# The low part of 22 of 64 weight tiles made by GpSimd instead of an adding DMA

## The chip, the core and the metric

The kernel runs on one core of a Trainium2 chip. The metric is the device time of an execution in microseconds, and the median of several executions. TensorE does the matrix products, VectorE and ScalarE the elementwise work, GpSimd elementwise work and the issue of DMAs that do arithmetic, SyncE (SP) the issue of the plain DMAs. Rows call them PE, DVE, ACT, POOL and SP; PEld is the loading of a stationary operand.

## What is computed

A retention layer (linear attention with a decaying state, batch 2, 8 heads, 768 positions, head width 64) gives 1536 rows of 512, and two feed-forward layers follow, each with a hidden width of 2048. All four weight matrices come in as 8-byte floats.

```python
state = gamma * state + outer(k[t], v[t]); y[t] = scale * q[t] @ state     # per batch and head
x = y.transpose(0, 2, 1, 3).reshape(1536, 512)
g = softplus(x @ w1_in);      x = g @ w1_out                               # first layer
h = x @ w2_in
out = (h * clip(h + 3, 0, 6) / 6) @ w2_out                                 # second layer
```

## The kernel before

**Matrix products in parts.** Every operand of the large products is kept as a high part, rounded to TensorE's fast format, and a low part, what the rounding left out. A product is three matmuls: high by high, high by low, low by high. For activations the parts are `hi` and `lo` (`x_hi` and `x_lo` between layers), for weights the two halves of one tile `w_parts`: `t[:, 0]` high, `t[:, 1]` low.

**Weights.** A matrix is cut into 16 tiles of 128 x 512 numbers, so there are 64. A tile is named by (m, o, f): layer m, o = 0 for the layer's first matrix and 1 for its second, f from 0 to 15. `fetch` has SyncE load the raw words of a tile into one of three `raw` buffers. `convert` makes 4-byte floats of them: ScalarE scales `raw` (L89), VectorE clamps it (L90, called the `raw` step below) and makes the word `w` in three steps, one with one input (L91) and two with two (L92, L93). `w` lies in one of two buffers, so the tile after next can start its `w` only when all that reads this one is done. Then the parts: ScalarE writes minus the rounded `w` to the low half (L95), a DMA that GpSimd issues adds `w` to it in place (L96), and ScalarE writes the rounded `w` to the high half (L97).

**The order of tiles.** `order` (L104 to L107) has four tiles of the first layer's first matrix, then one of the second and one of the first by turns, then the second layer's 32. `feed(n)` converts up to n of them; `done[1]` counts those converted.

**Steps and units.** The attention runs in 12 units of 128 rows (`unit`). The first four come alone, and the others stand ahead of the first steps of the feed-forward layers. A step (`step`) is one f for one chunk of 512 rows: `gemm1`, twelve matmuls of 512 columns, whose result goes through ScalarE and VectorE (`g`, `e`, then `hi` and `lo`), and `gemm2`, twelve matmuls with the `hi` and `lo` of two steps earlier (`LAG`). In chunk 0 of the first layer `lo` is made by GpSimd (L352), elsewhere by VectorE. Steps of chunk 0 feed the weight tiles, mostly two each. In a unit, VectorE multiplies the scores by a mask (`pt`, L213), on which TensorE's next products wait (`pt,vs`), and writes `on` and `bd`; GpSimd makes `vs`, `bd` and `x_lo`.

**What sets the order.** Each engine works through its own queue in order. Up to the first two tiles (`feed(2)`, L302) the queues stand as the code is written; after that (`nc.on = False`) a scheduler merges what the code gives into the queues when the program is built, by its own estimates of durations.

Of the kernel before, what the change touches and what calls it, by code (L numbers as in the profile page):

```python
# [10 lines left out]
F32 = mybir.dt.float32  # L11
F32R = mybir.dt.float32r
U32 = mybir.dt.uint32
AF = mybir.ActivationFunctionType
ALU = mybir.AluOpType
# [25 lines left out]
@with_exitstack  # L41
def kernel(ctx, tc, q, k, v, w1_in, w1_out, w2_in, w2_out, tq, tk, tc_, tg, out):
    nc = InOrder(tc)
    B, H, S, D = q.shape
    NT, DM = out.shape
    DFF = w1_in.shape[1]
    NP = H // 2
    KD = DM // P
    NF = DFF // P
    C = P  # L50
    NCH = S // C
    CH = 512
    chunks1 = [(0, 0, 512), (1, 0, 512), (2, 0, 512)]
    chunks2 = [(0, 0, 512), (1, 0, 512), (2, 0, 512)]
    LAG = 2
    EARLY = 4

    tc.nc.scalar.preload_act_table_set("softplus")

    xpool = ctx.enter_context(tc.tile_pool(name="xpool", bufs=1))  # L60
    x_hi = [xpool.tile([P, KD, CH], F32R, name=f"x_hi{c}") for c in range(NT // CH)]
    x_lo = [xpool.tile([P, KD, CH], F32R, name=f"x_lo{c}") for c in range(NT // CH)]

    win_p = ctx.enter_context(tc.tile_pool(name="win", bufs=NF))
    wout_p = ctx.enter_context(tc.tile_pool(name="wout", bufs=NF))
    psum = ctx.enter_context(tc.tile_pool(name="psum", bufs=1, space=PSUM))
    raw_p = ctx.enter_context(tc.tile_pool(name="raw", bufs=3))
    cv_p = ctx.enter_context(tc.tile_pool(name="cv", bufs=2))

    w_in_t, w_out_t, raws = {}, {}, {}  # L70
    words = {0: (w1_in.bitcast(U32), w1_out.bitcast(U32)), 1: (w2_in.bitcast(U32), w2_out.bitcast(U32))}

    def fetch(m, o, f):
        raw = raw_p.tile([P, CH, 2], U32, tag="raw", name="raw")
        src = words[m][o]
        if o:
            nc.sync.dma_start(out=raw.rearrange("p n t -> p (n t)"), in_=src[f * P:(f + 1) * P, :])
        else:
            nc.sync.dma_start(out=raw.rearrange("p (k n) t -> p k (n t)", k=KD),
                              in_=src[:, 2 * f * P:2 * (f + 1) * P].rearrange("(k p) f -> p k f", p=P))  # L80
        raws[m, o, f] = raw

    def convert(m, o, f):

        raw = raws.pop((m, o, f))
        low, y = raw[:, :, 0], raw[:, :, 1]

        w = cv_p.tile([P, CH], U32, tag="w", name="w")
        nc.scalar.activation(y.bitcast(F32), y.bitcast(F32), AF.Copy, scale=2.0 ** -112)  # L89
        nc.vector.tensor_scalar(y.bitcast(F32), y.bitcast(F32), -TOP, TOP, ALU.max, ALU.min)  # L90
        nc.vector.tensor_scalar(w, y, 3, None, ALU.logical_shift_left)  # L91
        nc.vector.scalar_tensor_tensor(w, y, 0x80000000, w, ALU.bitwise_and, ALU.bitwise_or)  # L92
        nc.vector.scalar_tensor_tensor(w, low, 29, w, ALU.logical_shift_right, ALU.bitwise_or)  # L93
        t = (wout_p if o else win_p).tile([P, 2, CH], F32R, tag="w", name="w_parts")
        nc.scalar.activation(t[:, 1], w.bitcast(F32), AF.Copy, scale=-1.0)  # L95
        nc.gpsimd.dma_start(out=t[:, 1].bitcast(F32), in_=w.bitcast(F32), accum_op=ALU.add)  # L96
        nc.scalar.activation(t[:, 0], w.bitcast(F32), AF.Copy)  # L97
        if o:
            w_out_t[m, f] = t
        else:  # L100
            w_in_t[m, f] = t.rearrange("p a (k n) -> p a k n", k=KD)

    NU = B * NCH
    order = [(0, 0, f) for f in range(EARLY)]  # L104
    for f in range(NF):
        order += [(0, 1, f)] + [(0, 0, f + EARLY)] * (f + EARLY < NF)
    order += [(1, 0, f) for f in range(NF)] + [(1, 1, f) for f in range(NF)]  # L107
    done = [0, 0]

    def fetch_weights(n):  # L110
        while done[0] < min(len(order), n):
            fetch(*order[done[0]])
            done[0] += 1

    def feed(n):

        n = min(n, len(order))
        while done[1] < n:
            fetch_weights(done[1] + (1 if nc.on else 2))
            convert(*order[done[1]])  # L120
            done[1] += 1

    banks = psum.tile([P, 8, CH], F32, name="banks")
    free = list(range(8))

    def bank(hold=False):

        i = free.pop(0)
        if not hold:
            free.append(i)  # L130
            return banks[:, i, :]
        return i, banks[:, i, :]

    def release(i):
        free.append(i)

    def first(f):
        return EARLY + 2 * (f + 1) - max(0, f + 1 + EARLY - NF)

    step, last, n_steps = moe(ctx, tc, nc, out, x_hi, x_lo, w_in_t, w_out_t, chunks1, chunks2, NF, KD, DM, CH, LAG, feed, first, bank, release)  # L140
    s = 0
    with ExitStack() as actx:
        unit = attention(actx, tc, nc, q, k, v, tq, tk, tc_, tg, x_hi, x_lo, CH, bank, feed, fetch_weights)
        for u in range(CH // P, NU):
            unit(u)
            step(s)
            s += 1
    while s < n_steps:
        step(s)
        s += 1  # L150
# [298 lines left out]
```

## Time and profile before

| | us |
|---|---|
| median of 3 runs | 633.73 (632.96 to 635.1) |
| the profiled execution | 632.11 |
| its span, first to last instruction | 630.3 |
| TensorE busy in the span | 600.6 (95%) |
| VectorE busy | 352.4 (56%) |
| ScalarE busy | 281.1 (45%) |
| GpSimd busy, DMA issues counted | 116.5 (18%) |
| mean granted TensorE clock | 0.984 of full speed |

The shares are means over the whole span; VectorE and GpSimd have most of their work in the first 200 us. The time outside the span is 1.8 us. A busy TensorE isn't TensorE at its peak: where its clock is granted at half, the same matmul is busy for longer.

### The profile page before, as it was taken

The page shows a single profiled execution, that of the slowest core. Times are in us where ns is not written, and L with a number is a line of the kernel's source. Part 1 is how long each engine was busy: PE and PEld are TensorE (multiplying, and loading weights), DVE is VectorE, ACT ScalarE, POOL GpSimd, SP SyncE. Part 2 cuts the span into 40 slices and gives each one's busy share as a digit, 9 for nine tenths or more (in the row PEclk, how much of TensorE's full clock was granted, in tenths as well). Part 3 has the DMA queues.
Part 4 walks back from the last instruction along what each step waited for, and adds up shares of the span by engine and source line. Part 5 has one row for each costly group of instructions (what it writes and reads, how often), then busy time and mean ns, then how long its engine had stood idle before and what let it go on. Part 6 is the DMA issues. An engine that isn't in the chain of part 4 may idle for free.

```text
span 630.3 us, 7793 instructions
## 1 busy us (share of the span) xinstructions
PE 600.6 (95%) x2963; PEld 493.1 (78%) x2963; DVE 352.4 (56%) x567; ACT 281.1 (45%) x481; POOL 116.5 (18%) x126
## 2 busy tenths in 40 slices
PE   7957979799989999999999999999999999999997
PEld 6846767678768888888887878888888888888886
DVE  4569988898856333357576789932232222422223
ACT  3327556667655333356556677832222222222221
POOL 1735655444420000011111122300000000000000
PEclk9979979799999999999999999999999999999999
DMA  9988986798750000025558688810010000100001
GB/s 193 227 230 222 255 212 152 185 214 203 168 131 1 0 1 0 1 43 125 113 138 216 151 203 218 198 33 1 0 68 0 1 0 2 68 0 1 0 1 67
DMA packets 70662, 63.70 MB, mean 101 GB/s; under 512 B 40160, under 2 KB 56800, under 8 KB 70624
## 3 DMA queue, kind: packets, MB, share of 16 engines
q1 hardware_dynamic: 61408, 46.42, 25.5%
q0 software_dynamic: 9216, 16.78, 16.1%
q8 instruction: 23, 0.38, 0.3%
q14 instruction: 15, 0.12, 0.1%
HBM read 43.26 MB, written 3.15 MB: 74 GB/s over the span
## 4 chain that ended last, share of the span: by engine, by line
PE 60%; DVE 10%; issue 6%; DMA 4%; ACT 4%; POOL 1%; DVEq 0%; POOLq 0%; ACTq 0%
PE banks L31 60%; DVE w L31 5%; DMA raw<-in_moe_w_in_dram 3%; DVE raw L31 2%; ACT w_parts L31 1%; DVE g L31 1%; ACT e L31 1%; DMA w_parts<-w 1%; DVE e L31 1%; ACT raw L31 1%; ACT hi L31 1%; POOL lo L31 1%; DVE lo L31 1%; DVE pt L31 0%; POOL w_parts L31 0%
## 5 line engine op out<-in xcount | busy, mean ns | idle before, releaser
L31 PE MATMUL banks<-x_hi,w_parts 128*128 128x512 f32 x768 | 255.2, 393 | 5.5 <-DMA w_parts<-w 5.5
L31 PEld LDWEIGHTS banks<-x_hi,w_parts 128*128 128x128 f32 x768 | 145.0, 189 | 36.4 <-DMA w_parts<-w 5.7
L31 PE MATMUL banks<-x_lo,w_parts 128*128 128x512 f32 x384 | 150.2, 391 | 0.0
L31 PE MATMUL banks<-hi,w_parts 128*128 128x512 f32 x384 | 127.0, 392 | 0.7 <-ACT hi L31 0.4
L31 PE MATMUL banks<-w_parts,hi 128*128 128x512 f32 (+1 forms) x386 | 118.5, 388 | 0.5 <-DVE g L31 0.5
L31 DVE SCALAR_TENSOR_TENSOR w<-raw,w 128x512 uint32<-128x512 uint32 x128 | 102.6, 801 | 2.0
L31 DVE SCALAR_TENSOR_TENSOR g<-e,banks 128x512 f32<-128x512 f32 x48 | 33.0, 688 | 125.2 <-ACT e L31 125.2
L31 POOL DMA_DIRECT2D w_parts<-w x64 | 55.9, 874 | 238.8 <-ACT w_parts L31 181.8
L31 ACT ACTIVATE w_parts<-w 128x512 fp32r<-128x512 f32 x128 | 74.3, 624 | 39.4 <-DVE w L31 38.7
L31 ACT ACTIVATE e<-banks,three 128x512 f32<-128x512 f32 x48 | 32.9, 686 | 127.6 <-PE banks L31 127.6
L31 ACT ACTIVATE hi<-g 128x512 fp32r<-128x512 f32 x96 | 60.6, 631 | 59.9 <-DVE g L31 59.1
L31 PEld LDWEIGHTS banks<-hi,w_parts 128*128 128x128 f32 x384 | 71.9, 188 | 17.1 <-ACT hi L31 1.6
L31 PEld LDWEIGHTS banks<-w_parts,hi 128*128 128x128 f32 x386 | 72.3, 188 | 15.8 <-DVE g L31 0.9
L31 PEld LDWEIGHTS banks<-x_lo,w_parts 128*128 128x128 f32 x384 | 72.7, 189 | 15.0 <-issue 0.3
L31 DVE TENSOR_TENSOR lo<-g,hi 128x512 fp32r<-128x512 f32 x80 | 55.3, 691 | 47.2 <-ACT hi L31 47.2
L31 PE MATMUL banks<-lo,w_parts 128*128 128x512 f32 x192 | 75.5, 393 | 2.3 <-POOL lo L31 2.1
L31 PE MATMUL banks<-w_parts,lo 128*128 128x512 f32 (+1 forms) x193 | 74.9, 388 | 0.0
L31 DVE SCALAR_TENSOR_TENSOR e<-g,banks 128x512 f32<-128x512 f32 x48 | 32.8, 683 | 33.0 <-ACT g L31 32.8
L31 ACT ACTIVATE raw<-raw 128x512 f32<-128x512 f32 x64 | 42.6, 668 | 17.0 <-DMA raw<-in_moe_w_in_dram 17.0
L31 DVE TENSOR_TENSOR g<-g,e 128x512 f32<-128x512 f32 x48 | 33.2, 691 | 27.4 <-ACT e L31 27.3
L31 PEld LDWEIGHTS banks<-lo,w_parts 128*128 128x128 f32 x192 | 36.0, 188 | 11.7 <-POOL lo L31 3.6
L31 ACT ACTIVATE g<-banks 128x512 f32<-128x512 f32 x48 | 28.3, 589 | 37.1 <-PE banks L31 36.7
(45 smaller groups left out, 413.8 us busy)
## 6 DMA issues: line engine op xcount, KB each, us to landing
raw<-in_moe_w_in_dram SPq DMA_DIRECT2D x32, 512.0 KB, 4.2
w_parts<-w POOLq DMA_DIRECT2D x64, 256.0 KB, 4.8
raw<-in_moe_w_out_dram SPq DMA_DIRECT2D x32, 512.0 KB, 4.5
q<-in_q_dram SPq DMA_DIRECT2D x12, 256.0 KB, 5.6
v<-in_v_dram SPq DMA_DIRECT2D x12, 256.0 KB, 4.9
k<-in_k_dram SPq DMA_DIRECT2D x11, 256.0 KB, 5.2
out_dram<-ob SPq DMA_DIRECT2D x11, 256.0 KB, 2.0
k<-in_k_dram SPq DMA_DIRECT2D x2, 128.0 KB, 2.7
```

Source lines behind the costliest of these rows:

```text
L31: ins = getattr(self.engine, op)(*args, **kwargs)
```

## The change

For the first eight tiles of `order` (`2 * EARLY` is 8: six of the first layer's first matrix, two of its second) and for all 16 of the first layer's second matrix, 22 tiles in all, ScalarE writes only the high half, and GpSimd subtracts it from `w` into the low half. The other 42 keep the adding DMA.

```diff
--- before.py
+++ after.py
@@ -92,9 +92,13 @@
         nc.vector.scalar_tensor_tensor(w, y, 0x80000000, w, ALU.bitwise_and, ALU.bitwise_or)
         nc.vector.scalar_tensor_tensor(w, low, 29, w, ALU.logical_shift_right, ALU.bitwise_or)
         t = (wout_p if o else win_p).tile([P, 2, CH], F32R, tag="w", name="w_parts")
-        nc.scalar.activation(t[:, 1], w.bitcast(F32), AF.Copy, scale=-1.0)
-        nc.gpsimd.dma_start(out=t[:, 1].bitcast(F32), in_=w.bitcast(F32), accum_op=ALU.add)
-        nc.scalar.activation(t[:, 0], w.bitcast(F32), AF.Copy)
+        if done[1] < 2 * EARLY or (m, o) == (0, 1):
+            nc.scalar.activation(t[:, 0], w.bitcast(F32), AF.Copy)
+            nc.gpsimd.tensor_tensor(t[:, 1], w.bitcast(F32), t[:, 0].bitcast(F32), ALU.subtract)
+        else:
+            nc.scalar.activation(t[:, 1], w.bitcast(F32), AF.Copy, scale=-1.0)
+            nc.gpsimd.dma_start(out=t[:, 1].bitcast(F32), in_=w.bitcast(F32), accum_op=ALU.add)
+            nc.scalar.activation(t[:, 0], w.bitcast(F32), AF.Copy)
         if o:
             w_out_t[m, f] = t
         else:
```

Durations and instructions change, and the scheduler orders the queues anew from the second tile on. Three places show how. A row is an instruction with what it writes and reads and what it waits for (the number behind a name is a buffer's, and differs between the two programs).

GpSimd's queue from the first weight tile on (`w_parts_384` is the first tile), before:

```order
L31 DMA w_parts_384<-w_378 128x512 [waits Activation_49]
L31 TENSOR_TENSOR vs_568<-v_410,tk_sb_110 128x512 [waits DMAHW3_49,Pool_49]
L31 TENSOR_TENSOR x_lo1_63<-on_457,x_hi1_60 128x4x128 [waits Activation_49]
L31 DMA w_parts_396<-w_390 128x512 [waits Activation_49]
L31 DMA w_parts_499<-w_493 128x512 [waits Activation_49]
L31 TENSOR_TENSOR lo_486<-g_480,hi_485 128x512 [waits Activation_49]
L31 TENSOR_TENSOR x_lo1_63<-on_582,x_hi1_60 128x4x128 [waits Activation_49]
L31 TENSOR_TENSOR vs_661<-v_427,tk_sb_110 128x512 [waits DMAHW1_49]
L31 DMA w_parts_511<-w_505 128x512 [waits Activation_49]
L31 TENSOR_TENSOR lo_605<-g_599,hi_604 128x512 [waits Activation_49]
```

and now:

```order
L31 TENSOR_TENSOR w_parts_384<-w_378,w_parts_384 128x512 [waits Activation_49,Pool_49]
L31 TENSOR_TENSOR x_lo1_63<-on_455,x_hi1_60 128x4x128 [waits Activation_49]
L31 TENSOR_TENSOR vs_562<-v_408,tk_sb_110 128x512 [waits DMAHW3_49]
L31 TENSOR_TENSOR w_parts_395<-w_389,w_parts_395 128x512 [waits Activation_49]
L31 TENSOR_TENSOR vs_653<-v_425,tk_sb_110 128x512 [waits DMAHW6_49]
L31 TENSOR_TENSOR lo_484<-g_478,hi_483 128x512 [waits Activation_49]
L31 TENSOR_TENSOR w_parts_497<-w_491,w_parts_497 128x512 [waits Activation_49]
L31 TENSOR_TENSOR x_lo1_63<-on_576,x_hi1_60 128x4x128 [waits Activation_49]
L31 TENSOR_TENSOR w_parts_508<-w_502,w_parts_508 128x512 [waits Activation_49]
L31 TENSOR_TENSOR lo_599<-g_593,hi_598 128x512 [waits Activation_49]
L31 TENSOR_TENSOR w_parts_519<-w_513,w_parts_519 128x512 [waits Activation_49]
```

Each DMA issue has become a subtraction, `vs` is made earlier, and the subtractions stand among `lo`, `x_lo` and `vs`.

TensorE's queue at the first large product, between the last of unit 3 and the scores of unit 4 (`qT`, `kT`), before:

```order
L31 MATMUL banks_80<-qT_439,kT_433 128x128 [waits Activation_49]
L31 MATMUL banks_80<-x_hi0_59,w_parts_384 128x512 [waits Activation_49]
L31 MATMUL banks_80<-x_lo0_62,w_parts_384 128x512 [waits Pool_49]
L31 MATMUL banks_80<-qT_439,kT_433 128x128 x7
L31 MATMUL banks_80<-x_hi0_59,w_parts_384 128x512 [waits DMASW0_49]
L31 MATMUL banks_80<-x_hi0_59,w_parts_384 128x512
```

and now:

```order
L31 MATMUL banks_80<-vs_352,k_151 128x128 x4
L31 MATMUL banks_80<-x_hi0_59,w_parts_384 128x512 [waits Activation_49]
L31 MATMUL banks_80<-x_lo0_62,w_parts_384 128x512 [waits Pool_49]
L31 MATMUL banks_80<-x_hi0_59,w_parts_384 128x512 [waits Pool_49]
L31 MATMUL banks_80<-x_hi0_59,w_parts_384 128x512
L31 MATMUL banks_80<-x_lo0_62,w_parts_384 128x512
```

The third matmul needs the low half. It waited for the DMA (`DMASW0`) and now waits for GpSimd (`Pool`); the eight score matmuls, which stood ahead of it, come after the product.

VectorE's queue around `pt` of unit 5 (`pt_632` before), before:

```order
L31 SCALAR_TENSOR_TENSOR w_493<-raw_489,w_493 128x512 [waits DVE_49]
L31 TENSOR_TENSOR g_480<-g_480,e_479 128x512 [waits Activation_49]
L31 TENSOR_TENSOR on_582<-banks_80,tq_sb_106 128x512 [waits PE_49,Pool_49]
L31 TENSOR_SCALAR w_505<-raw_491 128x512 [waits DVE_49]
L31 SCALAR_TENSOR_TENSOR w_505<-raw_491,w_505 128x512 [waits DVE_49] x2
L31 TENSOR_SCALAR raw_503<-raw_503 128x512 [waits DMAHW7_49,Activation_49]
L31 SCALAR_TENSOR_TENSOR e_598<-g_599,banks_80 128x512 [waits Activation_49]
L31 TENSOR_SCALAR w_517<-raw_503 128x512 [waits DMASW1_49,DVE_49]
L31 TENSOR_TENSOR pt_632<-banks_80,tm_sb_108 128x512 [waits PE_49]
L31 TENSOR_TENSOR g_599<-g_599,e_598 128x512 [waits Activation_49]
L31 TENSOR_TENSOR pt_632<-banks_80,tm_sb_108 128x512 [waits PE_49]
```

and now (`pt_624`):

```order
L31 TENSOR_TENSOR on_576<-banks_80,tq_sb_106 128x512 [waits PE_49,Pool_49]
L31 TENSOR_SCALAR w_502<-raw_489 128x512 [waits DVE_49,Pool_49]
L31 TENSOR_SCALAR raw_500<-raw_500 128x512 [waits DMAHW7_49,Activation_49]
L31 SCALAR_TENSOR_TENSOR w_502<-raw_489,w_502 128x512 [waits DVE_49]
L31 TENSOR_SCALAR w_513<-raw_500 128x512 [waits DVE_49]
L31 SCALAR_TENSOR_TENSOR w_502<-raw_489,w_502 128x512 [waits DVE_49]
L31 SCALAR_TENSOR_TENSOR e_592<-g_593,banks_80 128x512 [waits Activation_49]
L31 SCALAR_TENSOR_TENSOR w_513<-raw_500,w_513 128x512 [waits DVE_49]
L31 TENSOR_TENSOR pt_624<-banks_80,tm_sb_108 128x512 [waits PE_49]
L31 TENSOR_TENSOR g_593<-g_593,e_592 128x512 [waits Activation_49]
L31 SCALAR_TENSOR_TENSOR w_513<-raw_500,w_513 128x512 [waits DVE_49]
L31 TENSOR_TENSOR pt_624<-banks_80,tm_sb_108 128x512 [waits PE_49]
```

The `w` steps wait for GpSimd where they waited for a DMA queue (`DMASW`). Since the program's start ten two-input `w` steps now stand ahead of the second half of `pt`, where eight did.

## Rows read from the trace of the kernel before

**Rows 1.** Engines by stage: window, busy us (instructions) of PE, PEld, DVE, ACT, POOL; PEclk; DMA share; GB/s.

```profile
28.00:132.00 104.00, 84.35 (x568) 67.28 (x567) 87.83 (x135) 58.27 (x105) 53.23 (x52) 0.90 0.86 211
36.00:49.80 13.80, 8.29 (x58) 6.70 (x56) 8.03 (x13) 4.45 (x8) 3.02 (x3) 0.75 0.90 235
49.80:132.00 82.20, 69.56 (x453) 55.21 (x451) 73.29 (x113) 49.41 (x90) 45.05 (x44) 0.92 0.87 214
132.00:193.00 61.00, 58.67 (x253) 46.75 (x252) 48.54 (x77) 39.25 (x69) 23.90 (x22) 1.00 0.68 161
193.00:630.30 437.30, 432.73 (x1908) 357.16 (x1906) 202.15 (x332) 174.59 (x293) 27.83 (x32) 1.00 0.24 59
```

**Rows 2.** Timeline of TensorE: start, duration, instruction, and [idle before <- who ended it].

```profile
42.90 1.22 PE L31 MATMUL banks<-x_hi,w_parts 128*128 128x512 f32 x2 [5.51 <-DMA w_parts<-w]
...
50.41 0.62 PE L31 MATMUL banks<-x_hi,w_parts 128*128 128x512 f32 x2
...
58.45 0.43 PE L31 MATMUL banks<-pt,vs 128*64 128x128 f32 x2 [3.25 <-DVE pt L31]
...
115.28 2.08 PE L31 MATMUL banks<-qT,bd 128*128 128x128 f32 x8 [4.32 <-DVE pt L31]
```

**Rows 3.** Timeline of GpSimd, at the first tile and at 51 us.

```profile
34.60 1.02 POOL L31 DMA_DIRECT2D w_parts<-w  x1 [1.73 <-ACT w_parts L31]
...
50.85 0.85 POOL L31 DMA_DIRECT2D w_parts<-w  x1 [8.53 <-ACT w_parts L31]
51.56 1.46 POOL L31 TENSOR_TENSOR lo<-g,hi 128x512 fp32r<-128x512 f32 x1
52.81 1.43 POOL L31 TENSOR_TENSOR x_lo<-on,x_hi 128x512 fp32r<-128x512 f32 x1
54.05 1.20 POOL L31 TENSOR_TENSOR vs<-v,tk_sb 128x512 f32<-128x512 f32 x1
```

**Rows 4.** Timeline of VectorE, 43 to 88 us.

```profile
43.36 0.43 DVE L31 TENSOR_SCALAR w<-raw 128x512 uint32<-128x512 uint32 x1 [1.95 <-DMA w_parts<-w]
...
47.79 0.69 DVE L31 SCALAR_TENSOR_TENSOR e<-g,banks 128x512 f32<-128x512 f32 x1 [3.28 <-ACT g L31]
...
51.00 0.42 DVE L31 TENSOR_SCALAR w<-raw 128x512 uint32<-128x512 uint32 x1
51.46 5.07 DVE L31 SCALAR_TENSOR_TENSOR w<-raw,w 128x512 uint32<-128x512 uint32 x2
...
88.16 0.43 DVE L31 TENSOR_SCALAR w<-raw 128x512 uint32<-128x512 uint32 x1 [1.26 <-DMA w_parts<-w]
```

**Rows 5.** Groups of VectorE and GpSimd, 28 to 132 us: xcount, busy us, mean ns, idle before.

```profile
L31 DVE SCALAR_TENSOR_TENSOR w<-raw,w 128x512 uint32<-128x512 uint32 x40 | 36.4, 910 | 0.7
L31 DVE TENSOR_SCALAR raw<-raw 128x512 f32<-128x512 f32 x22 | 14.6, 665 | 0.5 <-ACT raw L31 0.4
L31 DVE TENSOR_SCALAR w<-raw 128x512 uint32<-128x512 uint32 x21 | 11.8, 561 | 3.4 <-DMA w_parts<-w 3.2
...
L31 POOL DMA_DIRECT2D w_parts<-w x20 | 17.6, 881 | 29.1 <-ACT w_parts L31 29.0
```

**Rows 6.** Timelines of ScalarE and VectorE in the later steps of chunk 0.

```profile
154.94 1.15 ACT L31 ACTIVATE w_parts<-w 128x512 fp32r<-128x512 f32 x2 [0.36 <-DVE w L31]
...
156.72 0.69 DVE L31 TENSOR_TENSOR g<-g,e 128x512 f32<-128x512 f32 x1 [0.87 <-ACT e L31]
...
163.87 0.69 DVE L31 TENSOR_TENSOR g<-g,e 128x512 f32<-128x512 f32 x1 [0.88 <-ACT e L31]
...
180.41 0.43 DVE L31 TENSOR_SCALAR w<-raw 128x512 uint32<-128x512 uint32 x1 [2.68 <-DMA w_parts<-w]
```

**Rows 7.** Timelines of GpSimd and VectorE at 165 us.

```profile
165.37 1.29 POOL L31 TENSOR_TENSOR lo<-g,hi 128x512 fp32r<-128x512 f32 x1 [1.38 <-ACT hi L31]
...
164.48 0.69 DVE L31 SCALAR_TENSOR_TENSOR w<-raw,w 128x512 uint32<-128x512 uint32 x1
...
165.42 1.80 DVE L31 SCALAR_TENSOR_TENSOR w<-raw,w 128x512 uint32<-128x512 uint32 x1
```

## The prediction

> **What bounds the kernel now.** Read first the table by stage, for which engine is full where [rows 1]. From 193 us to the end TensorE is busy 432.73 of 437.30 us at full granted clock: nothing the change touches lies there, and what counts is how much earlier or later TensorE gets to that point. Ahead of it TensorE loses 5.5 us of 13.8 (36 to 49.8 us), 12.6 of 82.2 (49.8 to 132, the attention units among the first layer's steps) and 2.3 of 61 (132 to 193, the other steps of chunk 0). In the middle stage VectorE is busy 73.29 of 82.20 us, 89%, and GpSimd 45.05.
>
> Then the timeline of TensorE, for what it waited for [rows 2]. The first large matmul with a low part stood 5.51 us for the adding DMA, from 37.39 to 42.90, and the pair behind the wait took 1.22 us where the same pair of the second tile, at 50.41, took 0.62. [...] The later waits, 3.25 us at 58.45 and 4.32 us at 115.28, end on VectorE's `pt`. From 50 us on it is VectorE that is late.
>
> Why VectorE is late stands in its own timeline beside GpSimd's. At 51.46 two `w` steps took 5.07 us; GpSimd ran `lo` from 51.56, `x_lo` from 52.81 and `vs` from 54.05, end 55.25, back to back [rows 3, 4]. Late in chunk 0, one such step took 1.80 us beside a `lo` of 1.29 us, and 0.69 us alone [rows 7]. So a GpSimd elementwise instruction that reads SBUF holds up VectorE's `raw` and `w` steps until it ends. The issue of an adding DMA doesn't: GpSimd issued one from 50.85 to 51.70 [rows 3], and the one-input `w` step at 51.00 beside it took 0.42 us [rows 4].
>
> **The change, part by part.**
>
> *What goes.* 22 adding DMAs (0.88 us of GpSimd each [rows 5] and 256 KB of traffic) and 22 negated copies on ScalarE. Moving bytes is worth nothing by itself: no raw tile is waited for on TensorE's path in these rows.
>
> *What comes.* 22 subtractions. They aren't in the trace; the nearest row has the same shape, engine and operation (`lo`, 1.29 us undisturbed, 1.46 us crowded [rows 3, 7]), so 1.4 us. In GpSimd's new order 13 of them stand up to the last attention unit and 9 after it.
>
> *The start.* The DMA was issued at 34.60 [rows 3], just after its copy. A subtraction that starts there ends at 36.0; TensorE got to the place at 37.39, behind eight score matmuls that now stand after the tile's matmuls, so it comes at 36 to 37. The wait of 5.51 us goes. VectorE gets back what hung on it: 1.95 us in which a `w` buffer waited for the DMA that read it, 3.28 us in which `e` waited for the first large product's ReLU, and later 1.26 us more for a buffer [rows 4]. **Gain: 6.5 us of VectorE's idle time.** From 50 us on VectorE sets the pace, so this counts, and TensorE's 5.5 us, with what the slow clock cost behind them, is the same time seen from the other side; I don't add it. What is late next is `pt` of unit 5: in the new order ten `w` steps stand ahead of its second half where eight stood.
>
> *The price on VectorE.* Between 28 and 132 us its 40 two-input `w` steps took 36.4 us where 0.69 each [rows 7] makes 27.6; the 22 `raw` steps 14.6 where 0.42 each (that of the one-input `w` step, of the same shape) makes 9.2; the 21 one-input `w` steps 11.8 where 8.8 would do [rows 4, 5]. Together 17 us held up. GpSimd was busy 53.23 us there [rows 1], of which 17.6 were DMA issues [rows 5]: 35.6 us of elementwise work, 32 instructions. That is 0.48 us of VectorE for each us on GpSimd, 0.67 us for a subtraction of 1.4. The bounds: nothing, if it runs while VectorE does `pt`, `on`, `e` or waits; 1.11 us where it meets a `w` step head on (1.80 less 0.69 [rows 7]); and at most its whole 1.4. I take 0.67, the mean over the same mixture in the same stage. **13 x 0.67 = 8.7 us lost.**
>
> [...]
>
> *The steps after the units.* There a step takes 7.15 us of VectorE (its `g` at 156.72 and the next at 163.87) against 5.44 us of matmuls (24, at 432.73 us for 1908 [rows 1]). In each, `g` waits 0.87 us for `e` on ScalarE, which stands behind a pair of copies of 1.15 us [rows 6]. Now this is one copy: it ends at 155.6, the subtraction runs 155.6 to 157.0, and `g`, with two inputs in SBUF, begins at 157.0, not 156.72. So the subtraction lies mostly under a wait that was there, and costs about 0.25 us in each of some seven such steps. **1.8 us lost.** If that cover weren't there, it would be 1.1 us each. At the end a `w` step waits 2.68 us for a buffer that an adding DMA holds [rows 6]; in the new order the last tiles are subtractions and the buffer is free sooner. TensorE lost 2.3 us in this whole stage [rows 1]; I count **1.0 us gained**, between 0 and 2.3.
>
> *Sum.* -6.5 + 8.7 + 1.8 - 1.0 = +3.0 us. The profiled execution took 632.1 us (span 630.3 and 1.8 around it), so 635.1; the median of the runs is 1.6 above the profiled one, so 636.7 against 633.7. One edit is a gain at a place that is easy to see and a price spread over 13 places, and the two are nearly equal: with a price c per subtraction before 132 us the sum is 13c + 1.8 - 7.5, zero at c = 0.44.
>
> **The rivals.**
>
> *The price finds cover (faster).* The subtraction comes 0.7 us after its tile's last `w` step, and if VectorE by then is in `pt`, `on`, `e` or waits for TensorE, it costs little. Between 28 and 132 us VectorE was idle 16.2 of 104 us [rows 1], of which the start's 6.5 are spent already; some 9.7 are left to hide in. At c = 0.2 and no loss in the late steps: 2.6 - 7.5 = -4.9, 628.8; at c = 0, 626.2. It decides below c = 0.44. For it: idle time is there, and GpSimd now needs no answer from a DMA queue that is 0.87 to 0.90 busy [rows 1]. Against it: in the new order what follows a tile's last `w` step is mostly the next tile's `raw` or `w` step.
>
> *Head on (slower by more).* Each meets a `w` step at 1.1 us, as at 165 us: 14.3 + 1.8 - 7.5 = +8.6, 642.3; with the full 1.4, 646.2. For it: in the first steps each unit gets two subtractions, and with `lo`, `x_lo` and `vs` GpSimd is then in bursts like that at 51 us, in which VectorE stood still through three instructions. Then `pt` is so late that TensorE's clock falls again, as after the 5.51 us.
>
> *Nothing measurable.* The 6 us won at the start are given back at `pt` of unit 5 and the next, and TensorE goes on as before: 633.7 within 1.9.
>
> **How the numbers follow.** About 0.3% (1.9 us) is what a measurement here can tell from no change. The forecast, c between 0.5 and 0.85, has its own range 634.5 to 639.1 and a chance of 0.36, of which 0.07 lies within 0.3%. Cover 0.34, head on 0.14, nothing 0.16. So faster 0.34, same 0.23, slower 0.43. Cases of both signs hold most of the chance, and the range reaches to both: 627 (c of about 0.06) to 643 (c of about 1.15), leaving out both ends, some 2 in 10.
>
> **What would show it.** Right: no wait for the first low part, the first large product some 6 us earlier; VectorE's mean `w` and `raw` steps in 28 to 132 us longer than 910 and 665 ns; TensorE's waits there on `pt`, as many us or more; seven late steps at about 7.4 us. Wrong: mean `w` steps no longer than before, or `pt` of unit 5 as much earlier as the first product is; then the start's gain arrives at 193 us whole and the kernel is faster. Wrong too if the late steps are nearer 8 us, since then the cover under `e` isn't there.

## The result and the profile after

| | before | after |
|---|---|---|
| median, us | 632.67 (six runs, 630.92 to 635.1) | 636.64 (six runs, 635.35 to 638.21) |
| ratio to before | | 1.0061 (95% interval 1.0034 to 1.0089) |
| the profiled execution, span, us | 632.11, 630.3 | 635.39, 633.6 |
| TensorE, VectorE, ScalarE, GpSimd busy, us | 600.6, 352.4, 281.1, 116.5 | 601.9, 366.4, 271.3, 130.0 |

The change makes the kernel slower, by 0.6%. The forecast was 636.7 us. The stages of the changed kernel, as in [rows 1] (busy time and instructions of PE, PEld, DVE, ACT, POOL, then TensorE's granted clock):

```profile
36.00:49.80 13.80, 13.13 (x105) 10.76 (x104) 13.57 (x19) 7.03 (x12) 8.32 (x7) 1.00 1.15 306
49.80:132.00 82.20, 63.10 (x402) 48.98 (x401) 75.60 (x109) 41.04 (x73) 47.36 (x40) 0.88 0.62 157
28.00:132.00 104.00, 82.68 (x564) 64.99 (x563) 96.44 (x137) 51.73 (x92) 61.62 (x52) 0.91 0.70 177
132.00:193.00 61.00, 57.44 (x240) 46.43 (x241) 52.92 (x74) 35.38 (x61) 28.96 (x22) 0.96 0.46 125
193.00:633.60 440.60, 436.11 (x1922) 359.86 (x1920) 203.07 (x333) 174.78 (x293) 27.85 (x32) 1.00 0.24 59
```

Between 36 and 49.8 us TensorE now loses 0.7 us where it lost 5.5, and its clock is granted in full (1.00) throughout. Before, the mean was 0.75 there [rows 1]; it was 0.50 from 40 to 44 us, where the wait ended, and the first pair of matmuls behind it took 1.22 us, that of the second tile 0.62 [rows 2]:

```profile
36.00:40.00 4.00, 1.39 (x16) 0.96 (x14) 3.87 (x6) 0.66 (x1) 2.14 (x2) 0.96 1.05 293
40.00:44.00 4.00, 1.10 (x3) 0.91 (x4) 2.02 (x5) 1.15 (x2) 0.88 (x1) 0.50 1.15 293
44.00:48.00 4.00, 4.00 (x19) 3.28 (x18) 0.72 (x2) 0.84 (x2) 0.00 (x0) 0.69 0.91 224
48.00:52.00 4.00, 4.00 (x33) 3.35 (x33) 3.59 (x7) 3.91 (x8) 1.15 (x2) 1.00 0.50 136
```

From 49.8 to 132 us TensorE loses 19.1 us where it lost 12.6, and VectorE, busy 87.83 us from 28 to 132 us before, is busy 96.44. TensorE's clock fell too, to 0.88 there and 0.96 behind it, where it was 0.92 and 1.00. After 193 us TensorE loses 4.5 us, as before (4.6), so the last row gives a ruler: before, 1908 matmuls were left at 193 us, now 1922. Each takes 0.227 us (436.11 / 1922), so the changed kernel is 3.2 us behind there, which is the whole difference of the spans (3.3). The ruler serves below too. In the runs whose last part is undisturbed it agrees with the span within about 1 us.

TensorE's timeline, at the first product and at its longest waits:

```profile
35.38 0.72 PE L31 MATMUL banks<-x_hi,w_parts 128*128 128x512 f32 x2
...
52.26 0.43 PE L31 MATMUL banks<-pt,vs 128*64 128x128 f32 x2 [1.53 <-DVE pt L31]
...
64.70 0.50 PE L31 MATMUL banks<-hi,w_parts 128*128 128x512 f32 x1 [2.44 <-ACT w_parts L31]
...
98.58 2.08 PE L31 MATMUL banks<-qT,bd 128*128 128x128 f32 x8 [4.79 <-DVE pt L31]
...
128.18 0.66 PE L31 MATMUL banks<-pt,vs 128*64 128x128 f32 x2 [4.17 <-DVE pt L31]
```

The first low part is there when TensorE comes to it, at 35.38 against 42.90 [rows 2]. The waits that follow end mostly on `pt`; the one at 64.70 ends on the high part of the fifth tile. What held VectorE up shows in its groups from 28 to 132 us, as in [rows 5]:

```profile
L31 DVE SCALAR_TENSOR_TENSOR w<-raw,w 128x512 uint32<-128x512 uint32 x42 | 40.4, 964 | 0.5
L31 DVE TENSOR_SCALAR w<-raw 128x512 uint32<-128x512 uint32 x21 | 16.4, 783 | 0.2
L31 DVE TENSOR_SCALAR raw<-raw 128x512 f32<-128x512 f32 x22 | 15.0, 683 | 0.0
...
L31 DVE TENSOR_TENSOR g<-g,e 128x512 f32<-128x512 f32 x7 | 5.8, 834 | 0.7 <-ACT e L31 0.7
```

Reckoned as in the prediction (0.69 us for a step with two inputs, 0.42 for one), these steps were held up 11.4 + 7.6 + 5.8 + 1.0 = 25.8 us; before it was 17.1. `pt`, `on` and `e` were not: their means are 0.68, 0.69 and 0.68 us, before 0.68, 0.69 and 0.69.

### The profile page after: what moved, and what is told of

Its sections match the earlier page's. It is cut to its first block, busy times and chain, and to the rows that moved or that the text cites. A ratio compares the mean times of both kernels' runs of the same rounds, so it can differ in the third digit from the quotient of the medians.

```text
span 633.6 us, 7713 instructions
## 1 busy us (share of the span) xinstructions
PE 601.9 (95%) x2963; PEld 494.0 (78%) x2963; DVE 366.4 (58%) x567; ACT 271.3 (43%) x459; POOL 130.0 (21%) x126
## 4 chain that ended last, share of the span: by engine, by line
PE 64%; DVE 20%; issue 7%; DMA 5%; ACT 4%; SPq 1%; POOL 0%; DVEq 0%; POOLq 0%; ACTq 0%
PE banks L31 64%; DVE w L31 11%; DVE raw L31 3%; DMA raw<-in_moe_w_in_dram 3%; DVE g L31 2%; DVE e L31 1%; DVE pt L31 1%; ACT e L31 1%; DMA w_parts<-w 1%; ACT raw L31 1%; DVE bd L31 1%; DMA q<-in_q_dram 1%; ACT w_parts L31 1%; ACT hi L31 1%; DVE lo L31 1%
## 5 line engine op out<-in xcount | busy, mean ns | idle before, releaser
L31 PE MATMUL banks<-x_hi,w_parts 128*128 128x512 f32 x768 | 255.0, 393 | 0.3 <-DVE e L31 0.2
L31 PEld LDWEIGHTS banks<-x_hi,w_parts 128*128 128x128 f32 x768 | 145.0, 189 | 31.2 <-issue 0.5
L31 PE MATMUL banks<-x_lo,w_parts 128*128 128x512 f32 x384 | 150.6, 392 | 0.0
L31 PE MATMUL banks<-hi,w_parts 128*128 128x512 f32 x384 | 128.0, 394 | 4.4 <-ACT w_parts L31 2.4
L31 PE MATMUL banks<-w_parts,hi 128*128 128x512 f32 (+1 forms) x386 | 118.4, 388 | 0.5 <-DVE g L31 0.5
L31 DVE SCALAR_TENSOR_TENSOR w<-raw,w 128x512 uint32<-128x512 uint32 x128 | 104.5, 818 | 1.8
L31 DVE SCALAR_TENSOR_TENSOR g<-e,banks 128x512 f32<-128x512 f32 x48 | 33.0, 688 | 125.2 <-ACT e L31 125.2
L31 PEld LDWEIGHTS banks<-hi,w_parts 128*128 128x128 f32 x384 | 72.7, 189 | 21.1 <-ACT w_parts L31 2.7
L31 ACT ACTIVATE e<-banks,three 128x512 f32<-128x512 f32 x48 | 32.9, 685 | 127.6 <-PE banks L31 127.6
L31 ACT ACTIVATE hi<-g 128x512 fp32r<-128x512 f32 x96 | 60.6, 631 | 62.6 <-DVE g L31 61.8
L31 ACT ACTIVATE w_parts<-w 128x512 fp32r<-128x512 f32 x106 | 62.6, 626 | 55.1 <-DVE w L31 45.1
L31 PEld LDWEIGHTS banks<-w_parts,hi 128*128 128x128 f32 x386 | 72.4, 188 | 15.8 <-DVE g L31 0.9
L31 PEld LDWEIGHTS banks<-x_lo,w_parts 128*128 128x128 f32 x384 | 72.6, 189 | 15.4 <-issue 0.7
L31 DVE TENSOR_TENSOR lo<-g,hi 128x512 fp32r<-128x512 f32 x80 | 55.3, 691 | 47.2 <-ACT hi L31 47.2
L31 POOL DMA_DIRECT2D w_parts<-w x42 | 37.0, 882 | 206.7 <-ACT w_parts L31 150.0
L31 PE MATMUL banks<-lo,w_parts 128*128 128x512 f32 x192 | 75.9, 395 | 2.3 <-POOL lo L31 2.1
L31 PE MATMUL banks<-w_parts,lo 128*128 128x512 f32 (+1 forms) x193 | 74.9, 388 | 0.0
L31 DVE SCALAR_TENSOR_TENSOR e<-g,banks 128x512 f32<-128x512 f32 x48 | 32.8, 683 | 33.5 <-ACT g L31 33.4
L31 DVE TENSOR_TENSOR g<-g,e 128x512 f32<-128x512 f32 x48 | 36.1, 753 | 24.6 <-ACT e L31 24.5
L31 ACT ACTIVATE raw<-raw 128x512 f32<-128x512 f32 x64 | 42.5, 668 | 13.6 <-DMA raw<-in_moe_w_in_dram 13.6
L31 PEld LDWEIGHTS banks<-lo,w_parts 128*128 128x128 f32 x192 | 36.5, 190 | 11.2 <-POOL lo L31 2.8
L31 ACT ACTIVATE g<-banks 128x512 f32<-128x512 f32 x48 | 28.3, 590 | 37.4 <-PE banks L31 37.3
```

What stands on the lines that cost most here:

```text
L31: ins = getattr(self.engine, op)(*args, **kwargs)
```

## The experiments

Theory A is the prediction's: the start gives back 6.5 us, and each subtraction on GpSimd holds up VectorE, which sets the pace, by 0.67 us. Rival B: what is won at the start is lost at the next `pt` anyway, and the 4 us are the price of all 22 subtractions. Rival C, later called the order theory: the scheduler's new order costs the time, not the held-up VectorE. Each run is compared with the kernel before on the same chip.

| run | tiles by subtraction | median, us | ratio to before, 95% interval |
|---|---|---|---|
| the change | 22 | 636.64 | 1.0061 [1.0034, 1.0089] |
| e1 | the first | 625.41 | 0.9897 [0.9865, 0.9929] |
| e2 | the first 8 | 626.22 | 0.9902 [0.987, 0.9933] |
| e3 | second matrix, 16 | 638.34 | 1.0093 [1.0059, 1.0127] |
| e4 | first layer, 32 | 645.68 | 1.0211 [1.0176, 1.0247] |
| e5 | none, 7 spare ones added | 639.62 | 1.0123 [1.0102, 1.0143] |
| e6 | 22, on VectorE | 623.58 | 0.9869 [0.9835, 0.9902] |
| e7 | the last 8 of the second matrix | 654.79 | 1.0345 [1.0312, 1.0379] |
| e8 | three | 623.12 | 0.9863 [0.9842, 0.9884] |
| e9 | 22 in the change's order, 21 narrow | 641.04 | 1.0146 [1.0113, 1.0178] |
| e10 | 22 in the change's order, on VectorE | 630.35 | 0.9977 [0.9958, 0.9996] |
| e11 | 22 in e6's order, on GpSimd | 631.29 | 0.9975 [0.9952, 0.9998] |
| e12 | 22 in the order of before | 650.35 | 1.0288 [1.0253, 1.0322] |

### e1 to e4: how many tiles, and which

```diff
-        if done[1] < 2 * EARLY or (m, o) == (0, 1):
+        if done[1] < 1:              # e1
+        if done[1] < 2 * EARLY:      # e2
+        if (m, o) == (0, 1):         # e3
+        if m == 0:                   # e4
```

> Only the first weight tile gets its low part by the subtraction, the other 63 keep the adding DMA. Theory A (the prediction's sum: the start gives back 6.5 us, each subtraction before 132 us costs 0.67): the one subtraction runs where nothing else is in its way, so about 6 us faster than before, 627 us against 632.7. Rival B (given back: VectorE's pt sets the pace from unit 5 on, so whatever is won at the start is lost there, and the 3.97 us by which the change is slower are the price of all 22 subtractions): no change, 632.7 within 1.9. Rival C (it is the scheduler's new order that costs the time, not VectorE being held up): the order is new here too, and the result can be on either side; nothing near 6 us is due.

> Only the first clause: eight tiles by subtraction, all eight before the last unit; the first layer's second matrix keeps the DMA but for its first two tiles. A: -6.5 + 8 x 0.67 = -1.1 us, so 631.6 us; mean two-input w step between 910 and 964 ns. B: 632.7 and up to 2 more. C: GpSimd's queue is the same as the changed kernel's up to the eighth subtraction, so the loss shows by then: 635 to 637, like the change.

> Only the second clause: the 16 tiles of the first layer's second matrix, seven of them up to the last unit, and the first four tiles keep the DMA, so the start is as before. A: no gain at the start, 7 x 0.67 = 4.7, late steps 1.8 lost, end 1.0 gained: +5.5 us, 638.2 us, slower than the full change. B: the price alone, spread over 22, so 16/22 of about 4 us: 635.6 us, not slower than the full change. C: no number is due; the first product's 5.5 us wait stays.

> All 32 tiles of the first layer by subtraction, about 18 of them up to the last unit and two in most later steps. A: -6.5 + 18 x 0.67 = +5.6; the later steps now hold two subtractions and a lo, the second of them without the cover of g's wait, so 0.25 + 0.67 to 1.1 in each of seven, some 7 us; end 1.0 gained: about +11.5 us, 644 us. B: 32/22 of 4 us: 638.5 us. C: no more than the full change, 636.6 us, if the number of subtractions isn't what costs.

As shares of 632.3 us, e1 is 6.5 us faster, e2 6.2 us faster, e3 5.9 slower and e4 13.3 slower. A gave about 6 faster, 1.1 faster, 5.5 slower and 11.5 slower. B falls with e1: the start's gain arrives whole. A fits e1, e3 and e4. In e2 it is off by 5 us: seven early subtractions more than e1 cost next to nothing. TensorE's timeline of e1 shows why:

```profile
45.55 0.74 PE L31 MATMUL banks<-x_hi,w_parts 128*128 128x512 f32 x2 [1.82 <-DMA w_parts<-w]
...
63.25 1.19 PE L31 MATMUL banks<-hi,w_parts 128*128 128x512 f32 x4 [2.52 <-DMA w_parts<-w]
```

With the first wait gone, TensorE stands before the adding DMAs of the second and the fifth tile, 4.3 us together. In e2 and in the changed kernel TensorE waits for no adding DMA in chunk 0. So the early subtractions had a second gain, which the trace of before could not show: there the pair of the second tile did not wait [rows 2]. It is less than 4.3 us: at the fifth tile both stand for the high part instead, which comes late from VectorE and ScalarE, 1.60 us in e2 and 2.44 us in the changed kernel (its row at 64.70).

### e8: only the three tiles that TensorE waits for

```diff
-        if done[1] < 2 * EARLY or (m, o) == (0, 1):
+        if done[1] in (0, 1, EARLY):
```

> Subtraction for three tiles: the first two of the first matrix and the first of the second, on whose DMAs TensorE waited 5.51 us (before) and 1.82 and 2.52 us (with the first tile alone by subtraction). A: two subtractions cost VectorE 1.3 us more than the first tile alone, and TensorE's 4.3 us of waits are worth only what VectorE had to wait behind them, so between 1 us slower and 3 us faster than 625.4: 622.4 to 626.7, and if the bound is VectorE alone, 626.7. Rival: TensorE's waits are each lost for good, 4.3 us, so 621 us.

e8 is 8.7 us faster than before, 2.2 more than e1, and within what A allowed (622.4 to 626.7), near its lower end: the two waits are gone but for 0.61 us at the fifth tile, for its high part, and 0.60 us for an adding DMA at another place, and two subtractions cost some of that. If each cost about 0.67 us, the two waits were worth some 3.5 us (an estimate; the order of e8 is its own).

### e5: the price alone

```diff
         nc.scalar.activation(t[:, 0], w.bitcast(F32), AF.Copy)
+        if (m, o) == (0, 1) and f < 7:
+            spare = cv_p.tile([P, CH], F32, tag="spare", name="spare")
+            nc.gpsimd.tensor_tensor(spare, w.bitcast(F32), t[:, 0].bitcast(F32), ALU.subtract)
```

> The kernel before, all its adding DMAs kept, with one more GpSimd subtraction of the same shape and operands for seven tiles (f below 7 of the first layer's second matrix), whose result goes to a spare buffer that nobody reads. No transfer goes, no engine waits for the new work. A (each subtraction holds VectorE up by 0.67 us, and VectorE sets the pace there): 7 x 0.67 = 4.7 us slower than before, 637.0 us against 632.3, with mean w steps longer than 910 ns. Rival C (GpSimd works beside VectorE at no price, and what the change costs comes from the order or from tiles that are ready later): 632.3 within 1.9, since GpSimd has time and nobody waits.

Seven subtractions that nobody waits for make the kernel 7.8 us slower (6.4 to 9.0), 1.1 us each (0.9 to 1.3) and more than A's 0.67. C, which gave no change, fails, and here the order can't be the cause: in the built program the other instructions of TensorE, VectorE and ScalarE stand in the order of before, one by one, and GpSimd's do but for one pair of neighbours. Reckoned as above, from 28 to 193 us VectorE is held up 31.7 us, 7.0 more than before. The group of GpSimd from 28 to 150 us:

```profile
L31 POOL TENSOR_TENSOR spare<-w,w_parts 128x512 f32<-128x512 f32 x7 | 10.5, 1502 | 0.1
```

### e7: only late tiles

```diff
-        if done[1] < 2 * EARLY or (m, o) == (0, 1):
+        if (m, o) == (0, 1) and f >= 8:
```

> Only the last eight tiles of the first layer's second matrix (f from 8) by subtraction: nearly all of them after the last unit, none at the start. The prediction's terms for the late steps: 1.8 lost and 1.0 gained, so +0.8 us, 633.1. What the traces of the changed kernel and of the one with the second matrix alone point to instead (from the tenth lo of chunk 0 to the end 2.1 and 1.8 us longer than before): about +2 us, 634.3. Nothing at all (the late subtractions lie under the wait for e, the burst at the end is covered): 632.3.

It is 21.8 us slower, which no theory gave (the profiled execution, 648.98 us, is the fastest of six). Most of the loss is not where the subtractions are: in the window from 193 us 1910 matmuls are left, two more than before, so 0.5 us behind. Further on TensorE stands idle for 14.8 us, where it was 4.6, and its matmuls take some 6 us longer at a clock of 0.99:

```profile
193.00:647.20 454.20, 439.39 (x1910) 357.82 (x1908) 202.13 (x331) 174.03 (x292) 28.18 (x32) 0.99 0.23 57
```

The reason is taken up behind e12. For the late steps, VectorE's `pt` of the last unit helps, in e7 and in the kernel before:

```profile
124.78 1.28 DVE L31 TENSOR_TENSOR pt<-banks,tm_sb 128x512 f32<-128x512 f32 x2
```

```profile
128.59 1.28 DVE L31 TENSOR_TENSOR pt<-banks,tm_sb 128x512 f32<-128x512 f32 x2
```

At that place e7 is 3.8 us ahead. Its change can't be the reason: its first subtraction starts at 131.12, and in the built programs the queues of TensorE, VectorE, ScalarE and GpSimd are the same up to there. So executions of one order can lie that far apart, for a reason that no run here singles out (TensorE's clock was granted 0.96 from 49.8 to 132 us in this one, 0.92 before). From there to 193 us e7 goes from 3.8 ahead to 0.5 behind: the stage with the eight late subtractions lost some 4 us against before.

### e6: on VectorE instead

```diff
-            nc.gpsimd.tensor_tensor(t[:, 1], w.bitcast(F32), t[:, 0].bitcast(F32), ALU.subtract)
+            nc.vector.tensor_tensor(t[:, 1], w.bitcast(F32), t[:, 0].bitcast(F32), ALU.subtract)
```

> The changed kernel with the 22 subtractions on VectorE (0.69 us each by its rows of the same shape) in place of GpSimd. A: held-up time and own time are about equal, 0.67 against 0.69 us, so before the last unit nothing changes; late in chunk 0 the subtraction no longer hides under g's wait, 0.69 against 0.25 us in seven steps, but the burst at the end goes: 636 to 640 us, against 636.6 for the change. Rival C (GpSimd's subtractions cost VectorE little): 13 x 0.69 = 9 us more work on the engine that sets the pace, so 643 us or more.

Both expectations fail: it is 8.3 us faster than before and, by the two ratios, 12 us faster than the change. VectorE does better with the 22 subtractions in its own queue than with GpSimd doing them. Whether that is the engine or the order, which the scheduler made anew, this run can't tell; the next four hold the order.

### e9 to e12: the order held

Each of these programs is built twice: first a reference, whose queues are read off, and then the program itself, with every instruction tied behind the one that precedes it in the reference's queue:

```diff
+                for a, b in zip(q, q[1:]):
+                    tc.add_manual_dep(b, a.name, mybir.DependencyInfo(
+                        mybir.DependencyClass.NoSync, mybir.DependencyReason.DATA), reason="order")
```

In e10 and e11 the subtractions alone are not tied, since they change engine. In the rows of these four, L40 is the line that L31 was. e9 also has (`REF` holds while the reference is built; the matmuls' operands change to match)

```diff
-            nc.gpsimd.tensor_tensor(t[:, 1], w.bitcast(F32), t[:, 0].bitcast(F32), ALU.subtract)
+            n = CH if REF or done[1] == 0 else P
+            nc.gpsimd.tensor_tensor(t[:, 1, :n], w.bitcast(F32)[:, :n], t[:, 0, :n].bitcast(F32), ALU.subtract)
```

> The order of the changed kernel is held on every engine; the 22 subtractions leave GpSimd's queue and stand in VectorE's, where the scheduler puts them among the other instructions in their held order. Held-up theory, with a price per subtraction on GpSimd well above the 0.69 us that VectorE takes for it itself: most of what the run with VectorE in the scheduler's own order won comes back, 624 to 629 us. Held-up theory with the price 0.67: 636 to 638. Order theory: the gain of that run was its order, so 636 to 640 us here.

> The other corner: the order of the run that had the subtractions on VectorE (623.6 us) is held on every engine, and the 22 subtractions are back on GpSimd. Held-up theory with a price well above 0.69: 633 to 640 us, the order doesn't help. Held-up theory with the price 0.67: as with VectorE, 623.6. Order theory: 623 to 626 us, since the order is that of the fast run and VectorE has 22 instructions less.

With the change and e6, these make a table of two by two, as ratios to before:

| | on GpSimd | on VectorE |
|---|---|---|
| order of the change | 1.0061 | 0.9977 (e10) |
| order of e6 | 0.9975 (e11) | 0.9869 (e6) |

From GpSimd to VectorE in one order: 5.3 us, or 6.7 in the other. From one order to the other on one engine: 5.4 or 6.8 us, each good to about 2 us. So engine and order both count, with shares of about the same size, and neither theory's range is met: e10 lies between 624 to 629 and 636 to 640, e11 between 623 to 626 and 633 to 640.

The share of the order is seen in TensorE's waits for `pt` from 28 to 193 us (total, times, longest), of the change, e10, e11 and e6. They are short in e6's order on either engine:

```profile
PE banks L31 <- DVE pt L31: 16.1, 10, 4.8
PE banks L40 <- DVE pt L40: 16.2, 9, 4.4
PE banks L40 <- DVE pt L40: 10.4, 7, 2.5
PE banks L31 <- DVE pt L31: 8.0, 6, 2.0
```

The share of the engine isn't VectorE's time: in e10 its steps are held up 23.8 us from 28 to 193 us, 15.6 less than in the change (39.4, rows below), but the 22 subtractions are 15.2 us of its own work. What gains the 5.3 us in one order was not tried. One place where the orders differ, late in chunk 0 on VectorE, in e6 and then in the changed kernel:

```profile
160.10 0.68 DVE L31 SCALAR_TENSOR_TENSOR e<-g,banks 128x512 f32<-128x512 f32 x1
160.69 0.68 DVE L31 SCALAR_TENSOR_TENSOR w<-raw,w 128x512 uint32<-128x512 uint32 x1
161.30 0.42 DVE L31 TENSOR_SCALAR w<-raw 128x512 uint32<-128x512 uint32 x1
161.63 0.42 DVE L31 TENSOR_SCALAR raw<-raw 128x512 f32<-128x512 f32 x1
161.97 0.68 DVE L31 TENSOR_TENSOR g<-g,e 128x512 f32<-128x512 f32 x1
```

```profile
155.94 0.68 DVE L31 SCALAR_TENSOR_TENSOR e<-g,banks 128x512 f32<-128x512 f32 x1
156.54 0.42 DVE L31 TENSOR_SCALAR w<-raw 128x512 uint32<-128x512 uint32 x1
157.32 1.35 DVE L31 TENSOR_TENSOR g<-g,e 128x512 f32<-128x512 f32 x1 [0.36 <-ACT e L31]
```

e6 puts three weight steps between `e` and `g`, and `g` waits for nothing; the change puts one there, and `g` waits 0.36 us and is then held up 0.66. In sum `g` waits 2.6 us from 132 to 193 us in both, so this place alone isn't the gain.

> Every engine's order is held to that of the changed kernel, instruction for instruction; 21 of the 22 subtractions (all but the first tile's) work on 128 of 512 columns only. The other 384 columns of these low parts are left out, and the matmuls that would read them read the high part's columns instead, so TensorE's work stays. Held-up theory (GpSimd's subtractions hold VectorE up for as long as they run): some two thirds of the price go, at 0.67 each for 13 and what the late ones cost some 6 to 8 us: 629 to 631 us. Order theory (the scheduler's new order costs the time): as the changed kernel, 636.6 us.

> The order of the kernel before is held on every engine, and the 22 tiles of the change get their low part by subtraction, each in the place where its DMA's issue stood in GpSimd's queue. Held-up theory: the start's wait for the DMA goes, the subtractions hold VectorE up as in the changed kernel: 632.3 + 3 = 635 us, with TensorE's first low part about 5 us earlier. Order theory: the start's gain stays whole, 626 to 627 us.

By their medians both are slower than the change, which no theory gave, but up to 193 us, where the change is made, the order theory fails and the held-up one stands, in e9 with about twice the 6 to 8 us that it gave. The windows from 193 us of e9 and of e12:

```profile
193.00:640.00 447.00, 429.74 (x1864) 350.31 (x1862) 195.53 (x321) 168.60 (x282) 27.89 (x32) 0.99 0.23 58
```

```profile
193.00:649.00 456.00, 440.20 (x1917) 359.08 (x1915) 204.01 (x333) 174.88 (x294) 28.56 (x32) 0.99 0.23 57
```

e9 has 1864 matmuls left there, 58 less than the changed kernel in the same order: 13.2 us. Its GpSimd had 17.4 us less to do (groups of GpSimd from 28 to 193 us, of the change and of e9):

```profile
L31 POOL TENSOR_TENSOR w_parts<-w,w_parts 128x512 fp32r<-128x512 f32 x22 | 30.3, 1377 | 26.9 <-ACT w_parts L31 26.9
```

```profile
L40 POOL TENSOR_TENSOR w_parts<-w,w_parts 128x128 fp32r<-128x128 f32 x21 | 11.6, 553 | 24.3 <-ACT w_parts L40 24.3
...
L40 POOL TENSOR_TENSOR w_parts<-w,w_parts 128x512 fp32r<-128x512 f32 x1 | 1.3, 1270 | 2.6 <-ACT w_parts L40 2.6
```

That is 0.76 us of TensorE for each us of GpSimd, where I had taken 0.48. It is a little nearer to the most that I allowed, the subtraction's whole length, than to that mean.

That it is VectorE which is freed shows in its groups from 28 to 193 us, of before, the change and e9:

```profile
L31 DVE SCALAR_TENSOR_TENSOR w<-raw,w 128x512 uint32<-128x512 uint32 x68 | 61.3, 901 | 1.0
L31 DVE TENSOR_SCALAR raw<-raw 128x512 f32<-128x512 f32 x37 | 20.9, 567 | 3.0 <-ACT raw L31 2.8
L31 DVE TENSOR_SCALAR w<-raw 128x512 uint32<-128x512 uint32 x34 | 19.3, 568 | 6.1 <-DMA w_parts<-w 5.9
```

```profile
L31 DVE SCALAR_TENSOR_TENSOR w<-raw,w 128x512 uint32<-128x512 uint32 x68 | 63.2, 932 | 0.8
L31 DVE TENSOR_SCALAR w<-raw 128x512 uint32<-128x512 uint32 x34 | 26.3, 776 | 0.2
L31 DVE TENSOR_SCALAR raw<-raw 128x512 f32<-128x512 f32 x37 | 23.7, 641 | 1.6 <-ACT raw L31 1.5
L31 DVE TENSOR_TENSOR g<-g,e 128x512 f32<-128x512 f32 x16 | 14.0, 874 | 3.2 <-ACT e L31 3.2
```

```profile
L40 DVE SCALAR_TENSOR_TENSOR w<-raw,w 128x512 uint32<-128x512 uint32 x68 | 61.2, 902 | 0.8
L40 DVE TENSOR_SCALAR w<-raw 128x512 uint32<-128x512 uint32 x34 | 20.2, 596 | 0.2
L40 DVE TENSOR_SCALAR raw<-raw 128x512 f32<-128x512 f32 x37 | 19.3, 521 | 1.1 <-ACT raw L40 1.0
```

Reckoned as above (`g` isn't held up before and in e9), that is 24.8 us held up before, 39.4 in the change and 24.0 in e9: 15.5 us less than in the change, for 13.2 us gained in the same order.

e12, with the order of before, has 1917 left, so it is 2.0 us behind before: the prediction's sum was +3.0. VectorE is held up 36.7 us there.

What e7, e9 and e12 lose after 193 us is in VectorE's groups from 270 to 430 us, where the second layer's tiles are converted, of the change and of e9:

```profile
L31 DVE TENSOR_SCALAR w<-raw 128x512 uint32<-128x512 uint32 x30 | 12.7, 422 | 5.4 <-DMA w_parts<-w 5.3
```

```profile
L40 DVE TENSOR_SCALAR w<-raw 128x512 uint32<-128x512 uint32 x29 | 12.4, 426 | 29.4 <-DMA w_parts<-w 29.3
```

The first `w` step waits for a buffer that an adding DMA still reads, 29 us in all, with the same order of instructions; in e7 and e12 it is 27 and 26 us, in the other runs 4 to 6. The difference is in the buffers. The addresses of `w` in the built programs, a letter for each, for the 32 tiles of either layer in the order of `order`:

```
before       ABACBACBACBACBACBACDBACDBACDBACD  ADADADABCABCABCABCDABCADBCADBCAD
the change   ABABCADBCADBCADBCADBCADBCDACBADB  ABABABACDBACDBACDBACDBACDBACDBAC
e7           ABACBACBACBACBACBACDBACDBACBDACB  DADADADADADADADADADADADADADADADA
e9           ABCABCABCABCABACDBACDBACDABDCBAC  DADADADADADADADADADADADADADADADA
e12          ABCABCABCABCABACBADCBADCBADBCADC  DADADADADADADADADADADADADADADADA
```

In the built programs `w` has four places in memory, not the two that the code asks for (and that the text on the kernel before names). In these three programs alone (e7, e9, e12) two places take turns through the whole second layer; in the other eleven they do for its first seven tiles, then three or four take turns. The three are the ones with the long waits. That the places cause them is read from this agreement; it was not tried by itself.

## Why the prediction was right

The direction and the mechanism were right. That the time fits so closely, 636.7 against 636.64 us, is luck twice over: the forecast was +3.0 us on a median of 633.7, and with three more runs that median is 632.67, so the change costs 4.0; and two terms of the sum were off against each other. Its steps:

- **The start, 6.5 us gained.** Right. The wait of 5.51 us went, and e1, with this step alone, is 6.5 us faster (4.5 to 8.5).
- **What is late next.** I named `pt` of unit 5 (`pt_632`; counted from 0, as `unit` counts, it is unit 6, and the scores that I gave to unit 4 are those of unit 5). Its halves came at 51.53 and 53.82 us in the changed kernel, 5 to 6 us earlier than before, where the first product came 7.5 us earlier. Had it come as much earlier as the product, I said, the kernel would be faster. That sign was badly chosen: the start's gain does arrive, as e1 shows, and the price is paid after it. What was late next were two more adding DMAs, 1.82 and 2.52 us in e1, worth some 3.5 us by e8. The sum has no term for them. The changed kernel has this gain at most in part, since it stands 2.44 us at the fifth tile.
- **13 subtractions at 0.67 us, 8.7 lost.** The mechanism is right, and so is the price: VectorE was held up 8.7 us more from 28 to 132 us, and 14.7 us more from 28 to 193, 0.67 for each of the 22. In other orders it is not the same: 0.54 in e12, 1.0 in e5. So the price depends on where in the order the subtraction falls. In TensorE's time it is less sure: by the last unit's `pt`, 127.36 us against 128.59, 14 subtractions had run (I had counted 13) and the kernel was 1.2 us ahead. Of 6.5 us gained, or up to 10.0 with the two DMAs, 5.3 to 8.8 were lost, 0.38 to 0.63 each.
- **The late steps, 1.8 lost and 1.0 gained.** Wrong in size, and for the end in sign. From the last unit's `pt` to the end the changed kernel lost 4.5 us (1.2 ahead, 3.3 behind), e7 4.3, e12 3.7 and e3 1.6, where the sum has 0.8. VectorE was held up 13.5 us from 132 to 193 us, 7.6 before. The cover under `g`'s wait is there as told: `g` is held 0.66 us, its wait falls from 0.87 to 0.36, and the step takes 7.28 us (157.32 to 164.60) against 7.15. The end is what failed. VectorE's wait of 2.68 us for the buffer is gone, but nothing is gained by it; the last subtractions come close upon `lo`. GpSimd and VectorE of the changed kernel there:

```profile
166.81 1.80 POOL L31 TENSOR_TENSOR lo<-g,hi 128x512 fp32r<-128x512 f32 x1 [1.42 <-ACT hi L31]
168.58 1.47 POOL L31 TENSOR_TENSOR w_parts<-w,w_parts 128x512 fp32r<-128x512 f32 x1
172.41 1.35 POOL L31 TENSOR_TENSOR w_parts<-w,w_parts 128x512 fp32r<-128x512 f32 x1 [2.35 <-ACT w_parts L31]
175.78 1.54 POOL L31 TENSOR_TENSOR lo<-g,hi 128x512 fp32r<-128x512 f32 x1 [2.02 <-ACT hi L31]
177.28 1.72 POOL L31 TENSOR_TENSOR w_parts<-w,w_parts 128x512 fp32r<-128x512 f32 x1
```

```profile
167.41 1.50 DVE L31 TENSOR_SCALAR w<-raw 128x512 uint32<-128x512 uint32 x1
168.82 1.51 DVE L31 TENSOR_SCALAR raw<-raw 128x512 f32<-128x512 f32 x1
...
176.22 3.33 DVE L31 SCALAR_TENSOR_TENSOR w<-raw,w 128x512 uint32<-128x512 uint32 x2
```

From one `lo` to the next it is 8.97 us here (166.81 to 175.78), 7.3 in the steps ahead.

So up to 3.5 us gained early and 3.7 us lost late were missed, and they nearly cancel. These figures are of single executions, which can lie 3.8 us apart in one order (e7); only the sign of the late loss is the same in all four. Of the rivals, *nothing measurable* falls with e1, which keeps the start's gain, and cover and head on are both seen in places, neither as the rule. The rival that the runs added is the order: held apart, it moves this kernel by 5 to 7 us, as much as the engine does. The sum had no term for it, and e12 shows why it did no harm: in the order of before the subtractions cost 2.0 us up to 193 us, in their own order 3.2. What stays open is which places in e6's order make `pt` come in time, and what the other engine gains in one order.

e1, e2, e6 and e8 beat both kernels clearly: 6.5, 6.2, 8.3 and 8.7 us faster than before.

## What to carry to other kernels

Replace a slow transfer only where something waits for it: with three subtractions (e8) the kernel is 8.7 us faster, with 22 it is 4 us slower, so the other 19 cost some 0.7 us each, because the engine that does them holds up the one that sets the pace (VectorE by 14.7 us more in the changed kernel than before, from 28 to 193 us). When a wait goes, look for the next one of its kind behind it, which the trace of before hides. Where a scheduler orders the queues, an edit can change order and buffers everywhere: hold the order to that of a reference before you give a difference of a few us to the edit.

## What the runs showed of the hardware

In the changed kernel GpSimd's elementwise instructions held up VectorE's steps with one input as well: `w` at 167.41 and `raw` at 168.82 us took 1.50 and 1.51 us beside GpSimd's `lo` and subtraction (1.80 and 1.47 us), 0.42 alone. And an instruction that nobody waits for, on an engine that is idle half the time (GpSimd was busy 53 of 104 us), cost 1.1 us of the kernel's time for 1.5 of its own, in an unchanged order (e5).
